# Where weight tiles wait before their conversion: other buffers, a filter load in four pieces, one write for two

## The chip, the cores and the metric

The kernel runs on one core of a Trainium2 chip. The metric is the device time of one execution in microseconds; a time given for a kernel is the median of several runs.

## What is computed

For 8 sequences of 3008 rows and 256 columns, a real Fourier transform along the rows, a product with a complex filter, the inverse transform, and then an MLP mixer over rows (token part) and columns (channel part):

```python
X = np.fft.rfft(x, axis=1)                      # x: (8, 3008, 256)
Y = X * (filt_r + 1j * filt_i)[None, :, :]      # 1505 x 256
x = np.fft.irfft(Y, n=3008, axis=1)             # float32
xt = x.transpose(0, 2, 1)
h = np.maximum(xt @ w_tok1, 0.0) @ w_tok2       # 3008 x 256, 256 x 3008
u = x + h.transpose(0, 2, 1)
out = u + np.maximum(u @ w_ch1, 0.0) @ w_ch2    # 256 x 1536, 1536 x 256
```

x and the filter are float32. The four weights are float64, and the kernel reads their bits.

## The kernel before

**The transform.** 3008 is 47 x 64, so the transform is done in two steps, each a matmul with a constant table. In `a_unit` (L283) two of 47 row groups of one batch are multiplied with the table wa, copied from PSUM by ScalarE (ACT) and written to a buffer in DRAM, z_tmp. In `b_unit` (L314), one of 32 frequencies k2 is read back (tile t2), multiplied with its table, and VectorE (DVE) makes the six operations of the complex product with the filter (L322 to L327). `bi_unit` (L330) does the first inverse step, ACT copies it to a tile t3, and t3 is written to a second buffer in DRAM, g_tmp. All of this is `dft` (L290), a generator that gives back control after each unit. The batches go in groups, `GROUPS`: batch 0 alone, then pairs.

**The mixer.** `mix` (L442) loads g_tmp as t4 tiles of four row groups, ends the inverse transform (L369) with a copy by DVE to a tile y (L372), does the token part with w1 and w2, and then twelve channel blocks for each of six row blocks (L404, L424). While a batch is mixed, the next group's `dft` runs between its steps.

**The weights.** A float64 number is made a float32 of equal value by `rounded` (L194) from its two 32-bit words: an ACT operation (L198), four DVE operations (L199, L200, L202, L204) and one sum per destination (L206). L204 is the last to read the staged words. There are 40 steps: 12 for w_tok1 (`w1_load`, two DMAs each), 16 for w_tok2 (`w2_load`), 6 for w_ch1 and 6 for w_ch2. Each is a generator in two halves: the first takes a staging tile and issues the load on POOL's queue, the second converts. `weights` (L252) runs the first halves of `AHEAD` = 5 steps, and then converts step i and issues step i + 5 in turn. A second token weight is reordered as it is written: three sums at L206, two of 23 row groups (184 columns) and one of the last row group (8 columns).

**Staging tiles** hold 128 x 512 eight-byte words, 4 KB a partition. They come from pool `t4p`, tag "t4", which has A // TC4 + 1 = 7 buffers; the mixer's t4 tiles come from the same pool and tag, six for a batch. Pools `up` (two buffers, tag "u"), `t2p` (three, "t2") and `t3p` (two, "t3") have tiles of 4 KB a partition too. A buffer is given to a new tile in the order of the program, and the instruction that writes the new tile waits until all that read or wrote the old one have ended.

**The order of the start** is written out by hand, at the end of the kernel. DVE clears the filter's tile `filt` (L475). `next(convert)` issues the loads of the first five steps, then `filt_load` (L173) issues eight DMAs on POOL's queue that gather the filter's rows: for the real and the imaginary part one of 24 partitions, two in falling order of rows (16 and 7 partitions), one for k2 = 0. Then batch 0's `dft` runs, and each of its first twelve units (the `a_unit`s) is followed by one conversion step. When it has ended, six `t4_load`s for batch 0 are issued on SP's queue, and then all conversions that are left, before the first `mix`:

```python
        for c in range(A // TC4):
            t4_load(0, c)
        for _ in convert:
            pass
```

Each engine takes its instructions in the order of the program, and so do the queues of SP, ACT and POOL.

Of the kernel before, what the change touches and what calls it, by code (L numbers as in the profile page):

```python
# [11 lines left out]
I64 = mybir.dt.int64  # L12
# [7 lines left out]
N1 = 47  # L20
N2 = 64
NF = N // 2 + 1
D = 256
P = 128
K2 = 32
A = 24
KR = 4 * A
HALF = 64
# [6 lines left out]
TC = DT // P  # L35
DC = 1536
JT = DC // P
DH = D // P
MT = 6
NG = 8  # L40
AHEAD = 5
GROUPS = ((0,), (1, 2), (3, 4), (5, 6), (7,))


# [65 lines left out]
def kernel(  # L110
# [11 lines left out]
    nc = tc.nc  # L122
# [12 lines left out]
    def pool(name, bufs, **kw):  # L135
        return ctx.enter_context(tc.tile_pool(name=name, bufs=bufs, **kw))
# [6 lines left out]
    t2p = pool("t2p", 3)  # L143
    pp = pool("pp", 2)
    t3p = pool("t3p", 2)
    t4p = pool("t4p", A // TC4 + 1)
    yp = pool("yp", 2)
    h1p = pool("h1p", 1)
    up = pool("up", 2)
# [12 lines left out]
    filt = glob.tile([P, K2, D], FP32, name="filt")  # L162
    w1 = glob.tile([P, A, DT], FP32, name="w1")
    w2 = glob.tile([P, TC, N], FP32, name="w2")
# [5 lines left out]
    def raw(src, row, ap):  # L170
        return bass.AP(tensor=src.tensor, offset=src.offset + row * D, ap=ap)

    def filt_load():  # L173
        for src, p0 in ((filt_r, 0), (filt_i, HALF)):
            nc.gpsimd.dma_start(filt[p0:p0 + A].rearrange("p a d -> p (a d)"),
                                raw(src, 0, [[64 * D, A], [1, K2 * D]]))
            lo = p0 + 32

            for j0, n in ((0, 16), (16, A - 1 - 16)):
                nc.gpsimd.dma_start(filt[lo + j0:lo + j0 + n, 1:K2, :],  # L180
                                    raw(src, 63 + 64 * j0, [[64 * D, n], [-D, K2 - 1], [1, D]]))
            nc.gpsimd.dma_start(filt[lo:lo + A, 0, :], raw(src, 32, [[64 * D, A], [1, D]]))

    def stage(n):
        return t4p.tile([P, n], I64, tag="t4", name="st")

    def rounded(st, n, parts):

        words = [st.bitcast(t).rearrange("p (n w) -> p n w", w=2)[:, 0:n] for t in (U32, FP32)]
        lo, hi, hi_f = words[0][:, :, 0], words[0][:, :, 1], words[1][:, :, 1]
        top = hp.tile([P, 512], FP32, tag="hh", name="top")[:, 0:n]
        rest = hp.tile([P, 512], FP32, tag="hh", name="rest")[:, 0:n]  # L194
        top_i, rest_i = top.bitcast(U32), rest.bitcast(U32)


        nc.scalar.activation(out=top, in_=hi_f, func=AF.Copy, scale=2.0 ** -112)  # L198
        nc.vector.tensor_scalar(out=top_i, in0=top_i, scalar1=3, scalar2=None, op0=ALU.logical_shift_left)  # L199
        nc.vector.scalar_tensor_tensor(out=top_i, in0=hi, scalar=0x80000000, in1=top_i,  # L200
                                       op0=ALU.bitwise_and, op1=ALU.bitwise_or)
        nc.vector.tensor_scalar(out=rest_i, in0=top_i, scalar1=0xFF800000, scalar2=None, op0=ALU.bitwise_and)  # L202

        nc.vector.scalar_tensor_tensor(out=rest, in0=lo, scalar=2.0 ** -52, in1=rest, op0=ALU.mult, op1=ALU.mult)  # L204
        for src, dst in parts:
            nc.vector.tensor_tensor(out=dst, in0=src(top), in1=src(rest), op=ALU.add)  # L206

    def w1_load(i):
        st = stage(512)
        rows = moe_w_tok1.rearrange("(n2 n1) t -> n2 n1 t", n1=N1)  # L210
        last = 2 * i + 2 == A
        if last:
            nc.gpsimd.memset(st.bitcast(U32)[HALF:P, 512:1024], 0)
        for h in range(2):
            n = 1 if last and h else 2
            lo = h * A + 2 * i
            nc.gpsimd.dma_start(st[h * HALF:(h + 1) * HALF, 0:n * DT].rearrange("p (a t) -> p a t", t=DT),
                                rows[:, lo:lo + n, :])
        yield
        rounded(st, 512, [(lambda v: v, w1[:, 2 * i:2 * i + 2, :].rearrange("p a t -> p (a t)"))])  # L220

    def w2_load(i):

        t, g = divmod(i, N2 // NG)
        n = NG * N1
        st = stage(512)
        nc.gpsimd.dma_start(st[:, 0:n], moe_w_tok2[ts(t, P), ts(g, n)])
        yield

        def some(lo, w):  # L230
            return lambda v: v.rearrange("p (n2 n1) -> p n1 n2", n1=N1)[:, lo:lo + w, :]

        w = A - 1
        dst = w2[:, t, 0:w * P].rearrange("p (a n2) -> p a n2", n2=P)
        rounded(st, n, [(some(h * A, w), dst[:, :, ds(h * HALF + g * NG, NG)]) for h in range(2)]
                + [(some(w, 1), w2[:, t, ds(w * P + g * NG, NG)].unsqueeze(1))])

    def wc1_load(i):
        c, q = divmod(i, DC // 512)
        st = stage(512)  # L240
        nc.gpsimd.dma_start(st, moe_w_ch1[ts(c, P), ts(q, 512)])
        yield
        rounded(st, 512, [(lambda v: v, wc1[:, c, ts(q, 512)])])

    def wc2_load(i):
        st = stage(512)
        nc.gpsimd.dma_start(st.rearrange("p (j d) -> p j d", d=D),
                            moe_w_ch2[ts(i, 2 * P), :].rearrange("(j p) d -> p j d", p=P))
        yield
        rounded(st, 512, [(lambda v: v, wc2[:, 2 * i:2 * i + 2, :].rearrange("p j d -> p (j d)"))])  # L250

    def weights():  # L252

        steps = ([w1_load(i) for i in range(A // 2)] + [w2_load(i) for i in range(TC * N2 // NG)]
                 + [wc1_load(c * (DC // 512) + q) for q in range(DC // 512) for c in range(DH)]
                 + [wc2_load(i) for i in range(JT // 2)])
        for s in steps[0:AHEAD]:
            next(s)
        yield
        for i, s in enumerate(steps):  # L260
            next(s, None)
            if i + AHEAD < len(steps):
                next(steps[i + AHEAD])
            yield


# [90 lines left out]
    t4 = {}  # L357

    def t4_load(b, c):
        t4[b, c] = t4p.tile([P, TC4, D], FP32, tag="t4", name="t4")  # L360
        nc.sync.dma_start(t4[b, c], rows_of(g_d, b)[:, ts(c, TC4), :])
# [80 lines left out]
    def mix(b, next_ready):  # L442
        h1 = token_hidden(b)
        wait = []
        uts, pos, hhs = {}, {}, {}

        def u_part(m, dh):
            if dh == 0:
                uts[m] = up.tile([P, DH, 512], FP32, tag="u", name="u")
            u_unit(b, m, h1, uts[m], dh)  # L450
            if dh == DH - 1 and b + 1 < B:
                wait.append(m)

        for dh in range(DH):
            u_part(0, dh)
        items = [(m, jt) for m in range(MT) for jt in range(JT)]
        for i in range(len(items) + 2):
            if i < len(items):
                m, jt = items[i]
                hhs[i] = hidden(uts[m], jt, width(m))  # L460
                if m + 1 < MT and jt in (5, 7):
                    u_part(m + 1, (jt - 5) // 2)
            if next_ready():
                for c in wait:
                    t4_load(b + 1, c)
                wait.clear()
            yield
            if i >= 2:
                m, jt = items[i - 2]
                down(b, m, jt, hhs.pop(i - 2), uts[m], pos.setdefault(m, []))  # L470

    with tc.manual_schedule():
        nc.sync.dma_start(wa, wa_d)
        nc.vector.memset(xlast[HALF:P, XC - 1, :], 0.0)
        nc.vector.memset(filt, 0.0)  # L475
        convert = weights()
        next(convert)
        filt_load()
        for i, _ in enumerate(dft(GROUPS[0])):
            if i == 0:  # L480
                for t, src in ((wai, wai_d), (ident, id_d)):
                    nc.scalar.dma_start(t, src)
            if i < A // 2:
                next(convert)
# [4 lines that stand above are left out]
        for bs, after in zip(GROUPS, GROUPS[1:] + ((),)):  # L489
            todo = dft(after) if after else iter(())  # L490
            done = not after
            for b in bs:
                def next_ready():
                    return b != bs[-1] or done

                for i, _ in enumerate(mix(b, next_ready)):
                    if not done and i % len(bs) == 0:
                        done = next(todo, "end") == "end"
            for _ in todo:
                raise AssertionError("the filter's steps don't fit beside the mixer's")  # L500
# [30 lines left out]
```

## Time and profile before

| | |
|---|---|
| median of 3 runs | 3232.15 us (3232.03 to 3232.48) |
| profiled execution: time | 3230.55 us |
| profiled execution: span | 3228.7 us |
| PE busy | 2941.8 us, 91% of the span |
| DVE busy | 843.9 us, 26% |
| ACT busy | 532.0 us, 16% |
| POOL busy | 134.7 us, 4% |
| mean granted TensorE clock | 0.999 |

The profile is one execution. Its span runs from the first to the last instruction, its time is the device time of the same execution, and the 1.85 us between them lie before and behind. The shares are averages over the whole span: the start, up to the first matmuls of the first `mix`, is told apart from the rest by windows of time. In rows of a timeline the first number is the start in us from the span's start, the second the duration, and the bracket at the end gives the engine's idle time before the row and what ended it. In a group of instructions the figures behind the bar are the busy time in us and the mean of one instruction in ns. An engine's name with a q (SPq, POOLq) is its queue's own work, issuing a DMA.

### The profile page before, as it was taken

The page shows a single profiled execution, that of the slowest core. Times are in us where ns is not written, and L with a number is a line of the kernel's source. Part 1 is how long each engine was busy: PE and PEld are TensorE (multiplying, and loading weights), DVE is VectorE, ACT ScalarE, POOL GpSimd, SP SyncE. Part 2 cuts the span into 40 slices and gives each one's busy share as a digit, 9 for nine tenths or more (in the row PEclk, how much of TensorE's full clock was granted, in tenths as well). Part 3 has the DMA queues.
Part 4 walks back from the last instruction along what each step waited for, and adds up shares of the span by engine and source line. Part 5 has one row for each costly group of instructions (what it writes and reads, how often), then busy time and mean ns, then how long its engine had stood idle before and what let it go on. Part 6 is the DMA issues. An engine that isn't in the chain of part 4 may idle for free.

```text
span 3228.7 us, 26261 instructions
## 1 busy us (share of the span) xinstructions
PE 2941.8 (91%) x10624; PEld 1876.0 (58%) x10624; DVE 843.9 (26%) x1442; ACT 532.0 (16%) x929; POOL 134.7 (4%) x257
## 2 busy tenths in 40 slices
PE   3610699999999999999999999999999999999999
PEld 0300466566666566666666566666666666666665
DVE  4954204751001434401001434401023330001000
ACT  1110022221121111111121111111111111111111
POOL 2000000000000000000000000000000000000000
PEclk9999999999999999999999999999999999999999
DMA  9332132330221212110221202110211101000000
GB/s 218 111 94 66 46 111 89 95 117 19 81 88 56 62 31 69 55 48 19 81 89 56 62 31 68 56 47 19 74 52 55 42 25 44 20 13 1 13 14 13
DMA packets 125096, 189.31 MB, mean 59 GB/s; under 512 B 16280, under 2 KB 84248, under 8 KB 124928
## 3 DMA queue, kind: packets, MB, share of 16 engines
q1 hardware_dynamic: 69520, 90.80, 9.4%
q0 software_dynamic: 14720, 46.35, 5.7%
q10 hardware_dynamic: 40736, 50.48, 4.7%
q8 instruction: 85, 1.39, 0.2%
q14 instruction: 35, 0.29, 0.0%
HBM read 112.59 MB, written 74.97 MB: 58 GB/s over the span
## 4 chain that ended last, share of the span: by engine, by line
PE 88%; DMA 5%; DVE 5%; issue 1%; ACT 1%; SPq 0%; POOL 0%; ACTq 0%; POOLq 0%
PE ps_po L424 31%; PE ps_pg L404 30%; PE ps_acc L378 5%; PE ps_acc L392 5%; PE ps_b L316 3%; PE ps_i L332 3%; PE ps_po L422 3%; PE ps_acc L397 3%; PE ps_a L369 3%; PE ps_a L285 2%; DMA x<-in_x_dram 2%; DMA st<-in_moe_w_ch_dram 1%; DMA st<-in_moe_w_tok_dram 1%; DVE rest L204 1%; DVE top L200 1%
## 5 line engine op out<-in xcount | busy, mean ns | idle before, releaser
L424 PE MATMUL ps_po<-wc,hh 128*128 128x256 f32 (+1 forms) x4608 | 1128.0, 381 | 0.0
L404 PE MATMUL ps_pg<-u,wc 128*128 128x512 f32 (+1 forms) x2304 | 1069.9, 587 | 0.0
L424 PEld LDWEIGHTS ps_po<-wc,hh 128*128 128x128 f32 (+1 forms) x4608 | 836.1, 188 | 311.2 <-issue 231.9
L407 ACT ACTIVATE hh<-ps_pg 128x512 f32<-128x512 f32 (+1 forms) x576 | 338.7, 588 | 1910.1 <-PE ps_pg L404 1844.0
L404 PEld LDWEIGHTS ps_pg<-u,wc 128*128 128x128 f32 x2304 | 430.5, 190 | 327.3 <-issue 296.4
L399 DVE COPY u<-ps_acc 128x512 f32<-128x512 f32 (+1 forms) x96 | 65.3, 680 | 792.3 <-PE ps_acc L397 792.3
L369 PE MATMUL ps_a<-t,wai 128*128 128x512 f32 x192 | 100.9, 607 | 182.9 <-DVE y L372 175.9
L440 POOL DMA_DIRECT2D out_dram<-o x192 | 100.1, 528 | 2781.1 <-ACT o L436 2730.8
L322 DVE TENSOR_TENSOR p<-ps_b,filt 64x512 f32<-64x512 f32 (+1 forms) x144 | 85.5, 594 | 437.2 <-PE ps_b L316 436.7
L392 PE MATMUL ps_acc<-w,h 128*128 128x512 f32 (+1 forms) x384 | 178.7, 588 | 11.8 <-DVE u L399 6.3
L436 DVE COPY o<-ps_po 128x512 f32<-128x512 f32 x40 | 27.6, 691 | 613.1 <-PE ps_po L424 613.0
L378 PE MATMUL ps_acc<-y,w 128*128 128x256 f32 x768 | 181.7, 381 | 0.0
L378 PEld LDWEIGHTS ps_acc<-y,w 128*128 128x128 f32 x768 | 147.1, 192 | 58.3 <-issue 42.7
L332 PE MATMUL ps_i<-p,wi 128*96 128x512 f32 (+1 forms) x320 | 153.7, 565 | 24.3 <-DVE p L327 14.5
L369 PEld LDWEIGHTS ps_a<-t,wai 128*128 128x128 f32 x192 | 36.3, 193 | 195.6 <-DVE y L372 183.3
L316 PE MATMUL ps_b<-t,wb 96*128 96x512 f32 (+1 forms) x288 | 134.9, 551 | 9.3 <-DMA t<-z_tmp 9.3
L422 PEld LDWEIGHTS ps_po<-ident,u 128*128 128x128 f32 (+1 forms) x768 | 114.3, 189 | 30.5 <-issue 23.1
L392 PEld LDWEIGHTS ps_acc<-w,h 128*128 128x128 f32 x384 | 71.6, 190 | 99.0 <-issue 80.6
L397 PEld LDWEIGHTS ps_acc<-wai,t 128*128 128x128 f32 x768 | 100.8, 192 | 44.2 <-issue 44.2
L422 PE MATMUL ps_po<-ident,u 128*128 128x128 f32 (+1 forms) x768 | 117.0, 275 | 0.0
L336 ACT COPY t<-ps_i 96x512 f32<-96x512 f32 (+1 forms) x160 | 79.4, 496 | 218.5 <-PE ps_i L332 216.2
L332 PEld LDWEIGHTS ps_i<-p,wi 128*96 128x96 f32 x320 | 54.1, 181 | 98.6 <-issue 93.4
(53 smaller groups left out, 1151.2 us busy)
## 6 DMA issues: line engine op xcount, KB each, us to landing
z_tmp<-t ACTq DMA_DIRECT2D x96, 256.0 KB, 2.5
t<-z_tmp SPq DMA_DIRECT2D x128, 192.0 KB, 3.4
g_tmp<-t ACTq DMA_DIRECT2D x128, 192.0 KB, 3.2
t<-g_tmp SPq DMA_DIRECT2D x48, 512.0 KB, 5.1
out_dram<-o POOLq DMA_DIRECT2D x184, 128.0 KB, 2.5
x<-in_x_dram SPq DMA_DIRECT2D x176, 128.0 KB, 3.3
wb<-wb_t SPq DMA_DIRECT2D x80, 96.0 KB, 2.0
wi<-wi_t SPq DMA_DIRECT2D x80, 96.0 KB, 2.0
```

The source lines that it names most:

```text
L316: nc.tensor.matmul(ps, wbs[k // WC][:, k % WC, :], t2s[k // KC][:, k % KC], start=True, stop=True)
L322: nc.vector.tensor_tensor(out=p1[re], in0=ps[re], in1=fr, op=ALU.mult)
L332: nc.tensor.matmul(ps[0:KR], wis[k // WC][:, k % WC, :], prods.pop(k), start=True, stop=True)
L369: nc.tensor.matmul(ps, wai, t4[b, c * XC // TC4][:, ds(c * XC % TC4, XC), :].rearrange("p a d -> p (a d)"), start=True, stop=True)
L378: nc.tensor.matmul(acc[:, t, :], w1[:, a, ts(t, P)], y[:, r, :], start=(a == 0 and t == 0), stop=(a == A - 1 and t == TC - 1))
L392: nc.tensor.matmul(ps[:, 0:w], h1[:, t, ts(dh, P)], w2[:, t, ds(m * 512, w)], start=(t == 0), stop=False)
L397: nc.tensor.matmul(ps[:, ds(q * P, n)], t4[b, c][:, r, ts(dh, P)], wai[:, 0:n], start=False, stop=(q == 3))
L404: nc.tensor.matmul(ps[:, 0:w], wc1[:, c, ts(jt, P)], ut[:, c, 0:w], start=(c == 0), stop=(c == DH - 1))
L407: nc.scalar.activation(out=hh[:, 0:w], in_=ps[:, 0:w], func=AF.Relu)
L422: nc.tensor.matmul(ps[:, ts(dh, P)], ut[:, dh, ds(q * P, n)], ident, start=(q % 2 == 0 and dh == 0), stop=False)
L424: nc.tensor.matmul(ps, hh[:, ds(q * P, n)], wc2[:, jt, :], start=False, stop=(end and q in (1, 2)))
L440: nc.gpsimd.dma_start(rows[:, lo:lo + n, :], o[h * HALF:(h + 1) * HALF, 0:n, :])
```

## The change

Four edits, all in the start of the kernel.

- `stage` takes its tiles from a list: the 12 first token weights from "t4" as before, then two from "u", then 26 from "t2" and "t3" by turns.
- `AHEAD` is 6 instead of 5, and `weights` is split: beside the first twelve conversions only steps up to 13 are issued (the first two second token weights); four more are issued after batch 0's spectral part and its t4 loads, and from there on step i + 6 is issued behind the conversion of step i.
- `filt_load` takes a range of k2 and is called four times by `weights`, for 8 values of k2 each, behind the conversions 0, 2, 4 and 6: eight DMAs for the first piece, six for each other.
- `w2_load` writes both runs of 23 row groups by one operation with a longer access pattern; the one for the last row group stays.

```diff
-AHEAD = 5
+AHEAD = 6
...
-    def filt_load():
+    def filt_load(k0, nk):
         for src, p0 in ((filt_r, 0), (filt_i, HALF)):
-            nc.gpsimd.dma_start(filt[p0:p0 + A].rearrange("p a d -> p (a d)"),
-                                raw(src, 0, [[64 * D, A], [1, K2 * D]]))
+            nc.gpsimd.dma_start(filt[p0:p0 + A, k0:k0 + nk, :], raw(src, k0, [[64 * D, A], [D, nk], [1, D]]))
             lo = p0 + 32
+            if k0 == 0:
+                nc.gpsimd.dma_start(filt[lo:lo + A, 0, :], raw(src, 32, [[64 * D, A], [1, D]]))
+            k = max(k0, 1)
 
             for j0, n in ((0, 16), (16, A - 1 - 16)):
-                nc.gpsimd.dma_start(filt[lo + j0:lo + j0 + n, 1:K2, :],
-                                    raw(src, 63 + 64 * j0, [[64 * D, n], [-D, K2 - 1], [1, D]]))
-            nc.gpsimd.dma_start(filt[lo:lo + A, 0, :], raw(src, 32, [[64 * D, A], [1, D]]))
+                nc.gpsimd.dma_start(filt[lo + j0:lo + j0 + n, k:k0 + nk, :],
+                                    raw(src, 64 * (j0 + 1) - k, [[64 * D, n], [-D, k0 + nk - k], [1, D]]))
+
+    stages = ([(t4p, "t4")] * (A // 2) + [(up, "u")] * 2
+              + [((t2p, "t2"), (t3p, "t3"))[i % 2] for i in range(TC * N2 // NG + JT - 2)])
 
     def stage(n):
-        return t4p.tile([P, n], I64, tag="t4", name="st")
+        where, tag = stages.pop(0)
+        return where.tile([P, n], I64, tag=tag, name="st")
...
         w = A - 1
-        dst = w2[:, t, 0:w * P].rearrange("p (a n2) -> p a n2", n2=P)
-        rounded(st, n, [(some(h * A, w), dst[:, :, ds(h * HALF + g * NG, NG)]) for h in range(2)]
-                + [(some(w, 1), w2[:, t, ds(w * P + g * NG, NG)].unsqueeze(1))])
+        dst = w2[:, t, 0:w * P].rearrange("p (a h n2) -> p h a n2", h=2, n2=HALF)
+
+        def both(v):
+            return bass.AP(tensor=v.tensor, offset=v.offset, ap=[v.ap[0], [A, 2], [1, w], [N1, NG]])
+
+        rounded(st, n, [(both, dst[:, :, :, ds(g * NG, NG)]), (some(w, 1), w2[:, t, ds(w * P + g * NG, NG)].unsqueeze(1))])
...
+        n1 = A // 2
         for s in steps[0:AHEAD]:
             next(s)
         yield
-        for i, s in enumerate(steps):
+        for i, s in enumerate(steps[0:n1]):
             next(s, None)
-            if i + AHEAD < len(steps):
+            if i + AHEAD < n1 + 2:
                 next(steps[i + AHEAD])
+            if i % 2 == 0 and i < 8:
+                filt_load(4 * i, 8)
+            yield
+        for s in steps[n1 + 2:n1 + AHEAD]:
+            next(s)
+        for i, s in enumerate(steps[n1:]):
+            next(s, None)
+            if n1 + i + AHEAD < len(steps):
+                next(steps[n1 + i + AHEAD])
             yield
...
         convert = weights()
         next(convert)
-        filt_load()
```

## The prediction

> **What bounds the kernel now.** I read the page's busy slices first, then busy time by 40 us windows, then the stretch where TensorE does nothing.
>
> ```profile
> span 3228.7 us, 26261 instructions
> PE   3610699999999999999999999999999999999999
> 0.00:40.00 40.00, 10.22 (x10) 2.50 (x10) 15.85 (x17) 5.94 (x9) 11.61 (x25) 1.00 1.00 181
> 40.00:80.00 40.00, 14.07 (x14) 3.58 (x14) 22.77 (x41) 9.69 (x16) 9.60 (x18) 1.00 0.98 252
> 80.00:120.00 40.00, 25.80 (x52) 14.00 (x52) 35.50 (x83) 4.41 (x12) 0.00 (x0) 1.00 0.37 113
> 240.00:280.00 40.00, 0.00 (x0) 0.00 (x0) 16.76 (x38) 2.93 (x5) 3.20 (x6) 1.00 0.23 66
> 360.00:400.00 40.00, 38.53 (x142) 25.34 (x141) 7.60 (x11) 3.29 (x6) 0.00 (x0) 1.00 0.06 19
> ```
>
> The windows give, behind the stretch, the busy time of PE, PEld, DVE, ACT and POOL with their instructions, the granted clock, the busy share of the DMA engines and GB/s. From about 350 us on TensorE is full and stays so; the change touches nothing there. Ahead of it lie three stages with three limits: to about 82 us the DMA engines are full (share 1.00 and 0.98), to about 172 us DVE is (35.5 of 40 us, the filter's products), and from there to 352 us nothing is: DVE 16.8 of 40, DMA 0.23, TensorE nothing. The timeline of DVE gives the edges, and the chain of waits shows what the third stage is made of.
>
> ```profile
> 85.91 0.42 DVE L322 TENSOR_TENSOR p<-ps_b,filt 64x256 f32<-64x256 f32 x1 [2.40 <-PE ps_b L316]
> ...
> 171.20 0.42 DVE L327 TENSOR_TENSOR p<-p,p 64x256 f32<-64x256 f32 x1
> 174.32 0.36 DVE L199 TENSOR_SCALAR top<-top 128x376 uint32<-128x376 uint32 x1 [2.70 <-ACT top L198]
> ...
> 176.27 0.92 DVE L206 TENSOR_TENSOR w<-top,rest 128x184 f32<-128x184 f32 x3
> 177.12 0.35 DVE L199 TENSOR_SCALAR top<-top 128x376 uint32<-128x376 uint32 x1
> ...
> 351.70 0.68 DVE L372 COPY y<-ps_a 128x512 f32<-128x512 f32 x1
> ```
>
> ```profile
> 195.40 0.56 DVE rest L204
> 195.99 0.51 issue
> 196.50 3.32 DMA st<-in_moe_w_tok_dram
> 199.90 0.55 ACT top L198
> ...
> 201.87 0.56 DVE rest L204
> ...
> 342.68 0.70 DVE rest L204
> ...
> 343.92 4.02 DMA st<-in_moe_w_ch_dram
> 348.02 0.67 ACT top L198
> ...
> 350.36 0.70 DVE rest L204
> ```
>
> One weight tile follows the other: DVE's last read of the staged tile (L204), half a microsecond, the next tile's load, ACT's and DVE's conversion, the next last read. A turn is 201.87 - 195.40 = 6.5 us for a second token weight and 350.36 - 342.68 = 7.7 us for a channel weight. The reason is in the code: a staged tile and the mixer's t4 tiles share seven buffers, six are given to batch 0's t4 loads before the remaining conversions, and one is left to rotate. POOL's timeline agrees: its first load of this stage waited 110 us and was released by a conversion's L204.
>
> ```profile
> 187.93 0.54 POOL L227 DMA_DIRECT2D st<-in_moe_w_tok_dram  x1 [109.98 <-DVE rest L204]
> ```
>
> **Term 1, the staging.** The stage converts 16 second token weights and 12 channel weights from 174.32 to 351.70, that is 177.4 us. After the change the tiles lie in two u buffers, three t2 and two t3 buffers, whose owners are idle between batch 0's spectral part and the mixer's first batch. Two tiles wait in u before the stage begins. The third and the fifth need t2 buffers whose last reader is TensorE, ahead of the last products at 171 us; the fourth and sixth need t3 buffers, free when their writes to DRAM have landed, a few us after those products, and they are due only three and five steps, 8 and 13 us, into the stage. From then on tile n needs the buffer of tile n-6 (t2) or n-4 (t3). The tighter one decides: from the last read of n-4 to the first DVE operation of n there are four pitches less the 1.9 us from the start of a conversion to the end of its L204 (174.32 to 176.27, where L206 begins), so 4 x 2.7 - 1.9 = 8.9 us. A load needs, by the turn above, from L204's end at 195.96 to ACT's end at 200.45, 4.5 us (5.3 for a channel weight, 343.38 to 348.69). That leaves 3.6 us or more: DVE no longer waits, and the stage lasts as long as DVE's work. If the cover went, by a landing of more than 4.0 + 3.6 = 7.6 us, each four steps would pay the excess.
>
> What a step costs DVE without waiting: 177.12 - 174.32 = 2.80 us for a second token weight. For a tile of 512 columns the first weights, which run the same five operations, show it back to back:
>
> ```profile
> 67.83 0.42 DVE L199 TENSOR_SCALAR top<-top 128x512 uint32<-128x512 uint32 x1
> 68.17 0.54 POOL L227 DMA_DIRECT2D st<-in_moe_w_tok_dram  x1 [1.03 <-DVE w L206]
> 70.81 0.42 DVE L199 TENSOR_SCALAR top<-top 128x512 uint32<-128x512 uint32 x1
> ```
>
> 2.98 us. ACT's part (0.55, 0.67) runs a step ahead on its own engine.
>
> **Term 2, one write for two.** Two operations of 184 columns become one of 368; the one of 8 stays.
>
> ```profile
> L206 DVE TENSOR_TENSOR w<-top,rest 128x184 f32<-128x184 f32 x32 | 13.5, 465 | 0.5
> L206 DVE TENSOR_TENSOR wc<-top,rest 128x512 f32<-128x512 f32 x12 | 8.3, 691 | 0.4
> L206 DVE TENSOR_TENSOR w<-top,rest 128x8 f32<-128x8 f32 x16 | 2.7, 166 | 0.0
> ```
>
> From 8 to 184 columns the strided operation grows by 299 ns, 1.70 ns a column; by that the merged one is 166 + 360 x 1.70 = 778 ns instead of 2 x 465 = 930, but neighbours overlap (465 + 465 + 166 = 1.10 us of work took 0.92, so 0.09 at each of two seams) and one seam goes, which leaves 0.06 us. By the contiguous row (691 ns for 512 columns, 1.04 ns a column) it would be 541 ns and the saving 0.3 us. The trace has no operation with so long an access pattern; I let a penalty take it to -0.1. I take 0.06, because the strided row is the same access: 2.74 us a step. Sixteen steps: 1 us, bounds -1.6 and 5.
>
> The stage is then 16 x 2.74 + 12 x 2.98 = 79.6 us instead of 177.4: 97.8 us less. At its end the same first y copy follows. Batch 0's t4 loads no longer compete for buffers; the spectral part keeps DVE's 85.7 us (85.91 to 171.62).
>
> **Term 3, the first stage.** The load of the filter becomes 26 DMAs instead of 8 and moves behind the loads of first weights, on POOL's queue; three of five second token weights leave the stage.
>
> ```profile
> DMA packets 7797, 18.19 MB, mean 214 GB/s; under 512 B 1455, under 2 KB 2523, under 8 KB 7747
> st<-in_moe_w_tok_dram POOLq DMA_DIRECT2D x23, 256.0 KB, 11.6
> st<-in_moe_w_tok_dram POOLq DMA_DIRECT2D x5, 376.0 KB, 7.5
> filt<-in_filt_i_dram POOLq DMA_DIRECT2D x1, 217.0 KB, 37.1
> ...
> 1.28 4.28 POOL L217 DMA_DIRECT2D st<-in_moe_w_tok_dram  x8 [0.82 <-POOLq L515]
> 6.02 0.52 POOL L217 DMA_DIRECT2D st<-in_moe_w_tok_dram  x1 [0.46 <-DMA st<-in_moe_w_tok_dram]
> ...
> 20.31 0.53 POOL L182 DMA_DIRECT2D filt<-in_filt_i_dram  x1 [1.94 <-DMA st<-in_moe_w_tok_dram]
> ...
> 55.31 1.02 POOL L217 DMA_DIRECT2D st<-in_moe_w_tok_dram  x2 [2.33 <-DMA filt<-in_filt_i_dram]
> ```
>
> The first four rows are of the DMA view from 0 to 85 us (count, KB each, us to landing), the others POOL's timeline. With the engines full, bytes set the stage: 3 x 376 KB = 1.16 MB less, at the stage's mean of 214 GB/s 5.4 us, at the 252 of its second half 4.6. I take 5. The filter's bytes are the same; what pieces do to their rate this trace does not show, so I bound it. Better: between 20 and 50 us, where the filter passes, six windows of 5 us move 104, 122, 135, 211, 150 and 155 GB/s, and 253 before them.
>
> ```profile
> 15.00:20.00 5.00, 1.50 (x2) 0.00 (x0) 1.90 (x4) 0.00 (x0) 1.91 (x3) 1.00 1.19 253
> 20.00:25.00 5.00, 0.00 (x0) 0.00 (x0) 0.00 (x0) 0.00 (x0) 0.53 (x1) 1.00 0.99 104
> ...
> 45.00:50.00 5.00, 2.05 (x2) 0.50 (x2) 0.00 (x0) 0.00 (x0) 0.51 (x1) 1.00 0.90 155
> ```
>
> At 253 the same 4.4 MB would take 17 us instead of 30, so 13 us more gain. Worse: POOL has at most eight loads in flight (eight leave at once, the ninth waits for a landing). Before, 24 + 8 + 5 = 37 loads pass, after 24 + 26 + 2 = 52; if a landing stays at 11.6 us whatever the size, 15 x 11.6 / 8 = 22 us are added. I stay with bytes, as the share of the DMA engines is full throughout, and count the extra issues (0.5 us each of POOL, which idles) at nothing. The pieces are due at the spectral part's units 0, 8, 16 and 24, spaced 8 x 2.7 us, and none is near its time.
>
> The Trainium skill, DMA: Bandwidth & Descriptors, "Anatomy of one DMA", puts a fixed cost of about 2 us on each DMA and so speaks against pieces: 18 more would be 36 us one behind another, or 4.5 us with eight in flight; by the latter the sum below would come to 99 instead of 103. The trace shows the eight in flight, so the former can't be the case.
>
> **The sum.** 98 + 5 = 103 us. The profiled execution took 3230.55 us (span 3228.7), 1.6 below the median of 3232.15; it gives 3127.5, and as a median of runs 3129.
>
> **The rivals.** (a) The pieces mix better with x and first weights: 13 us more, 3116. For it: engines full at half the rate. Against: the same few partitions are written. Chance 0.13. (b) The eight in flight bind: 22 us on top, no 5 saved: 3156 at the end, 3129 to 3156 on the way. For it: POOL waits for landings in the whole stage. Against: less in flight lands sooner. Chance 0.13. (c) POOL's loads cannot be prepared while DVE works without pause: the six staged tiles are used up, DVE waits 4.5 us, and so on; 22 further tiles in groups of six are 3.7 waits, 17 us: 3146. Against it: the POOL row at 68.17 stands inside a dense DVE step, takes 0.54 like the one at 187.93 beside an idle DVE, and the step keeps its 2.98. Chance 0.05. The Trainium skill, SBUF — State Buffer, "SBUF: two separate sides", states such a lock between VectorE and GpSimd's descriptors; by that row the trace doesn't show it here. (d) Slower: each filter piece stands in POOL's queue ahead of a first weight that ACT must convert before it copies the next x unit. If a piece landed as late as the whole does (37.1 us), four would take 148 us where the filter now takes 35 (20.31 to 55.31): 113 lost, 98 won, 3247. It decides from (98 + 35) / 4 = 33 us a piece. For it: 37.1 us for 217 KB is queue, not bytes. Against: that queue was the filter itself. Chance 0.02. (e) The change doesn't do what it says: the t2 or t3 buffers come free too late or are rotated one at a time, and the third stage keeps its turns: 3227 to 3232. The code gives five buffers by turns; chance 0.02.
>
> **How the numbers follow.** The likeliest case has the rest, 0.65: 3129, by itself 3122 to 3136. The range 3115 to 3144 takes in (a) and the near half of (b), and leaves out the far half, most of (c), (d) and (e): under 2 in 10. About 0.2% is what a measurement of this kernel can tell from no change, 6.5 us. Faster beyond it: all but (d) and (e), 0.96; same 0.02, slower 0.02.
>
> **What would show it.** DVE without gaps from the end of the spectral part (about 169 us) to the first y copy near 249, steps of about 2.7 and 2.98 us; POOL's loads there issued in bunches and not each released by the L204 just before; one L206 of 368 columns near 0.78 us; the first L322 near 81 us instead of 85.91; from the first y copy on the same 2877 us to the end. Wrong would be: gaps of DVE released by loads of st in that stage (c, e), or a first L322 at 90 us or later (b, d) or at 72 or earlier (a).

## The result, and the profile after

The changed kernel takes 3117.07 us (median of 4 runs, 3114.72 to 3118.63) against 3232.32 of the kernel before (4 runs): ratio 0.9642, 95% interval 0.9626 to 0.9659. Forecast were 3129 and a range of 3115 to 3144. The gain is 115 us where 103 were expected; the sign, the main term and its size held, the third term was three times as large.

The profiled execution took 3114.72 us, its span is 3112.9. The windows of the start answer to those of before (busy time of PE, PEld, DVE, ACT and POOL, granted clock, DMA share, GB/s):

```profile
0.00:40.00 40.00, 17.82 (x18) 4.30 (x18) 25.24 (x34) 9.57 (x15) 19.18 (x38) 0.98 0.98 255
40.00:80.00 40.00, 14.19 (x22) 5.88 (x22) 27.14 (x54) 7.29 (x13) 11.00 (x19) 0.50 0.77 203
80.00:120.00 40.00, 29.87 (x60) 16.01 (x60) 37.73 (x90) 5.51 (x15) 0.00 (x0) 0.50 0.35 105
160.00:200.00 40.00, 2.07 (x2) 0.50 (x2) 38.04 (x88) 8.24 (x15) 7.00 (x14) 0.50 0.71 239
200.00:240.00 40.00, 1.63 (x2) 0.84 (x3) 36.57 (x66) 7.36 (x11) 5.96 (x9) 0.50 0.35 123
240.00:280.00 40.00, 38.53 (x145) 27.15 (x144) 8.98 (x13) 0.60 (x1) 0.00 (x0) 0.96 0.00 0
```

The third stage has a limit now: DVE is busy 38.0 and 36.6 of 40 us where it was 16.8. And the first stage moves 255 GB/s in its first 40 us where it moved 181, at the same full share of the DMA engines. DVE's timeline gives the edges (L340, L345, L204, L211 and L390 are L322, L327, L199, L206 and L372 of before):

```profile
69.25 0.42 DVE L340 TENSOR_TENSOR p<-ps_b,filt 64x256 f32<-64x256 f32 x1 [6.49 <-PE ps_b L334]
...
154.62 0.42 DVE L345 TENSOR_TENSOR p<-p,p 64x256 f32<-64x256 f32 x1
157.74 0.36 DVE L204 TENSOR_SCALAR top<-top 128x376 uint32<-128x376 uint32 x1 [2.70 <-ACT top L203]
...
159.69 0.86 DVE L211 TENSOR_TENSOR w<-top,rest 128x368 f32<-128x368 f32 x2
160.47 0.38 DVE L204 TENSOR_SCALAR top<-top 128x376 uint32<-128x376 uint32 x1
...
237.63 0.68 DVE L390 COPY y<-ps_a 128x512 f32<-128x512 f32 x1
```

Between the two profiles the span is 115.8 us shorter (3228.7 to 3112.9), and it parts so: the first filter product 16.7 us earlier (85.91 to 69.25); from there to the first conversion no change (88.41 and 88.49 us); the conversions 97.5 us shorter (177.38 to 79.89); from the first y copy to the end 1.7 us shorter (2877.0 to 2875.3). POOL's timeline of the third stage shows the loads in pairs, each pair released by one L209 (L204 of before), some 5.5 us apart, which is two conversions:

```profile
168.43 1.06 POOL L232 DMA_DIRECT2D st<-in_moe_w_tok_dram  x2 [7.73 <-DVE rest L209]
173.94 1.06 POOL L232 DMA_DIRECT2D st<-in_moe_w_tok_dram  x2 [4.45 <-DVE rest L209]
179.47 1.06 POOL L232 DMA_DIRECT2D st<-in_moe_w_tok_dram  x2 [4.46 <-DVE rest L209]
```

Why the pieces of the filter were worth 12 us more than forecast was the open question. One theory was bytes (three weight tiles fewer), the rivals were the form of the transfers, their size and their place.

### The profile page after: what moved, and what is told of

The parts are those of the page before. It is cut to its first block, busy times and chain, and to the rows that moved or that the text cites. A ratio compares the mean times of both kernels' runs of the same rounds, so it can differ in the third digit from the quotient of the medians.

```text
span 3112.9 us, 26266 instructions
## 1 busy us (share of the span) xinstructions
PE 2941.5 (94%) x10624; PEld 1876.1 (60%) x10624; DVE 841.6 (27%) x1426; ACT 532.3 (17%) x929; POOL 145.3 (5%) x275
## 2 busy tenths in 40 slices
DMA packets 125576, 189.31 MB, mean 61 GB/s; under 512 B 16616, under 2 KB 84584, under 8 KB 125264
## 4 chain that ended last, share of the span: by engine, by line
PE 92%; DVE 5%; DMA 2%; issue 1%; ACT 0%; POOL 0%; POOLq 0%; ACTq 0%; SPq 0%; DVEq 0%
PE ps_po L442 33%; PE ps_pg L422 32%; PE ps_acc L396 5%; PE ps_acc L410 5%; PE ps_b L334 3%; PE ps_i L350 3%; PE ps_po L440 3%; PE ps_acc L415 3%; PE ps_a L387 3%; PE ps_a L303 2%; DMA st<-in_moe_w_tok_dram 1%; DMA z_tmp<-t 1%; DVE rest L209 1%; DVE top L205 1%; DVE p L343 0%
## 5 line engine op out<-in xcount | busy, mean ns | idle before, releaser
L458 POOL DMA_DIRECT2D out_dram<-o x192 | 100.1, 528 | 2782.8 <-ACT o L454 2771.0
L340 DVE TENSOR_TENSOR p<-ps_b,filt 64x512 f32<-64x512 f32 (+1 forms) x144 | 85.5, 594 | 441.3 <-PE ps_b L334 440.8
L387 PE MATMUL ps_a<-t,wai 128*128 128x512 f32 x192 | 100.9, 607 | 85.4 <-DVE y L390 78.6
L415 PEld LDWEIGHTS ps_acc<-wai,t 128*128 128x128 f32 x768 | 100.8, 192 | 44.2 <-issue 44.2
L390 DVE COPY y<-ps_a 128x512 f32<-128x512 f32 x96 | 66.3, 691 | 164.5 <-PE ps_a L387 163.8
```

The lines of the kernel that those rows point to most:

```text
L340: nc.vector.tensor_tensor(out=p1[re], in0=ps[re], in1=fr, op=ALU.mult)
L387: nc.tensor.matmul(ps, wai, t4[b, c * XC // TC4][:, ds(c * XC % TC4, XC), :].rearrange("p a d -> p (a d)"), start=True, stop=True)
L415: nc.tensor.matmul(ps[:, ds(q * P, n)], t4[b, c][:, r, ts(dh, P)], wai[:, 0:n], start=False, stop=(q == 3))
L458: nc.gpsimd.dma_start(rows[:, lo:lo + n, :], o[h * HALF:(h + 1) * HALF, 0:n, :])
```

## The experiments

Where a run has several times, its difference is to the kernel before on the same chip. The first filter product of one profile is a figure with a spread: four profiles of kernels whose first stage is the same (the changed one, the one with three sums, the one with two buffers, the one with the mixer beside) have it at 69.2, 70.7, 72.8 and 73.3 us, and four that load the filter whole, told below, at 82.0 to 85.0. Differences of less than 4 us in it say nothing by themselves.

**Whole filter, old place.** The staging is new, the load of the filter old.

```diff
-            if i % 2 == 0 and i < 8:
-                filt_load(4 * i, 8)
...
         next(convert)
+        filt_load()
```

> The changed kernel, but the filter is loaded whole by its old eight DMAs, ahead of the first weights' conversions as before. In question is why the first filter product (L322 before, L340 after) came 16.7 us earlier (85.91 to 69.2 us) where 5 were forecast. Bytes alone (three second token weights fewer in this stage): it stays near 69 us, total near 3117. The filter's form or place: near 81 us (85.9 less the 5 of the bytes), total near 3129. Either way the conversions behind the spectral part stay at 80 us without gaps.

3128.50 us (4 runs), before 3229.86: ratio 0.9688, 0.9674 to 0.9703. First product at 83.5 us, conversions 79.9 us. The new staging (with the merged write) gives 101 us without the pieces. The first product comes 2.4 us earlier than before; that is less than the spread, so it doesn't size the bytes of three weight tiles, but it is far from 16.7. Form or place of the load makes the rest.

**All pieces, old place.**

```diff
         next(convert)
+        for k0 in range(0, K2, 8):
+            filt_load(k0, 8)
```

> The changed kernel, but all four filter pieces (26 DMAs) are issued at the old place, ahead of all conversions. If the form of the pieces (shorter runs, no 32 KB packets in the way of the x units) made the gain: first product near 69 to 72 us, total near 3117 to 3120. If their place between the first weights did: near 81 us, total near 3129. If the number of DMAs in flight binds, later than that, near 90.

3121.44 us (4 runs), ratio 0.9667, 0.9652 to 0.9681; first product at 75.6 us. So 26 DMAs instead of 8 at the same place win 8 us in the profile and 7 in time (3128.50 to 3121.44, on the same chip). The place between the first weights' conversions wins 2 to 6 more by the profiles, which the spread leaves open; the run with three sums, which has the pieces there, is 4.7 us faster on the same chip, but it was timed once.

**Only the filter.** The kernel before with the pieces between the conversions.

```diff
                 next(steps[i + AHEAD])
+            if i % 2 == 0 and i < 8:
+                filt_load(4 * i, 8)
             yield
...
-        filt_load()
```

> The kernel before with the filter in four pieces between the conversions and nothing else: old staging, AHEAD 5, three sums. If the filter's form or place makes the other 12 us: first product near 74 us, total near 3220. If the gain comes from fewer bytes: near 86, total near 3232. The third stage keeps its turns of 6.5 and 7.7 us.

3217.62 us (5 runs), ratio 0.9961, 0.9947 to 0.9975: 12.2 us less, by itself. First product at 77.6 us, 8.3 earlier than before; the rest of the profile's gain of 11.7 us is not in the first stage: the conversions take 175.15 us instead of 177.38, for which no run shows a reason, and the time behind the first y copy is 1.3 us shorter, which is taken up below. With the 101.4 of the staging the two parts sum to 113.6 of the whole change's 115.3.

The windows from 10 to 60 us show what the pieces do. First the kernel before, then the one with the whole filter at its old place, with all pieces there, and the changed one:

```profile
10.00:60.00 50.00, 15.01 (x15) 4.00 (x16) 15.68 (x28) 7.57 (x13) 10.48 (x19) 1.00 1.02 190
```

```profile
10.00:60.00 50.00, 15.68 (x16) 4.01 (x16) 17.49 (x30) 7.25 (x13) 9.56 (x17) 1.00 1.03 188
```

```profile
10.00:60.00 50.00, 18.45 (x18) 4.51 (x18) 20.27 (x35) 9.86 (x17) 21.96 (x40) 1.00 1.03 236
```

```profile
10.00:60.00 50.00, 21.91 (x22) 5.30 (x22) 32.53 (x56) 14.24 (x24) 23.97 (x42) 0.79 1.03 274
```

The share of the DMA engines is 1.02 or 1.03 in all four, what they move goes from 188 to 274 GB/s. A full share is time in which packets are under way, not a rate.

**Three sums.**

```diff
-        rounded(st, n, [(both, dst[:, :, :, ds(g * NG, NG)]), (some(w, 1), w2[:, t, ds(w * P + g * NG, NG)].unsqueeze(1))])
+        rounded(st, n, [(some(h * A, w), dst[:, :, ds(h * HALF + g * NG, NG)]) for h in range(2)]
+                + [(some(w, 1), w2[:, t, ds(w * P + g * NG, NG)].unsqueeze(1))])
```

> The changed kernel with the second token weights written by three sums as before. Step of a second token weight 2.79 us instead of 2.76; the first y copy 0.5 to 1 us later from the start of the conversions. By the contiguous row it would be 0.3 us a step, 5 us.

The conversions take 80.4 us (159.25 to 239.66) instead of 79.9: the merged operation is worth 0.5 us. In the changed kernel's groups it costs 785 ns against two of 184 columns at 465:

```profile
L211 DVE TENSOR_TENSOR w<-top,rest 128x368 f32<-128x368 f32 x16 | 12.6, 785 | 0.6
...
L211 DVE TENSOR_TENSOR w<-top,rest 128x8 f32<-128x8 f32 x16 | 2.7, 170 | 0.0
```

The longer pattern costs as much a column as the shorter one, 1.70 ns, so only one start of an operation is saved.

**Whole filter in rows of 1 KB.**

```diff
         next(convert)
+        filt_load(0, K2)
```

> As the run with the filter whole and ahead of the conversions (first product at 83.5 us), but its two DMAs of 24 partitions are written as rows of 1 KB instead of runs of 32 KB; eight DMAs, same bytes, same place. If the 32 KB runs stand in the way of the other transfers, the first product comes near 75.6 us as with the pieces at that place. If the number of pieces makes those 8 us, it stays near 83.

First product at 82.0 us, 3129.45 us (one run). The rows are only in the way the code writes the load: over the whole execution this kernel and the one with the whole filter at its old place move the same 125096 packets, 124928 of them under 8 KB. The long runs are still there, so this run does not test them and is one more measure of the whole load. The run with the pieces in another order, below, does: it moves the packets of the pieces (125576, 125264 under 8 KB) and is as slow.

**Whole filter behind the first conversion.**

```diff
-            if i % 2 == 0 and i < 8:
-                filt_load(4 * i, 8)
+            if i == 0:
+                filt_load()
```

> The changed kernel with the filter loaded whole by its old eight DMAs, but behind the first conversion, where the first piece was. If the place alone makes 6 us (75.6 to 69.2 between pieces first and pieces between): first product near 77 us. If the place helps only because pieces alternate with first weights: near 83 us.

First product at 82.8 us, 3129.05 us (one run). The place by itself is worth nothing that the spread lets one see; if it helps, it is only where pieces alternate with first weights.

**The same pieces in another order.** What is left is that pieces are smaller, or that small DMAs of different partitions follow one another. This run keeps size, number and place and changes the order alone:

```diff
+            for k0 in range(0, K2, 8):
+                nc.gpsimd.dma_start(filt[p0:p0 + A, k0:k0 + 8, :], raw(src, k0, [[64 * D, A], [D, 8], [1, D]]))
...
+            for j0, n in ((0, 16), (16, A - 1 - 16)):
+                for k0 in range(0, K2, 8):
+                    k = max(k0, 1)
+                    nc.gpsimd.dma_start(filt[lo + j0:lo + j0 + n, k:k0 + 8, :],
```

> The same 26 filter DMAs at the same place as in the run with all pieces first (first product at 75.6 us), but in another order: all that write the same partitions stand together (24 partitions of the real part four times, then its 16, its 7, then the imaginary part), as the whole filter's eight DMAs do. If what counts is that the DMAs in flight at one time write different partitions: first product near 82 us, total near 3128. If smaller DMAs by themselves make the gain: near 75.6 us, total near 3121.

3130.96 us (4 runs; before 3231.80; ratio 0.9688, 0.9672 to 0.9704), first product at 84.6 us. In the order of this run the 26 DMAs are as slow as the eight; in the other they win 8 to 9 us. By time the two orders won 108.4 and 100.8 us on their own chips, 7.6 apart; the ends of the two intervals overlap, so it is the trace that decides. The window from 10 to 60 us has the rate of the whole filter, not that of the pieces:

```profile
10.00:60.00 50.00, 16.37 (x16) 4.02 (x16) 17.48 (x30) 7.67 (x13) 17.15 (x32) 1.00 1.02 194
```

The first product does not wait for the filter itself here: DVE converts without a gap up to it. What comes late are the first weights queued behind the filter. POOL issues the first of them at these times, with all pieces first and then in this run:

```profile
45.35 0.56 POOL L222 DMA_DIRECT2D st<-in_moe_w_tok_dram  x1 [0.20 <-issue]
```

```profile
54.72 0.58 POOL L222 DMA_DIRECT2D st<-in_moe_w_tok_dram  x1 [0.39 <-DMA filt<-in_filt_i_dram]
```

The rows of the DMA view for the 24 partitions (count, KB each, us to landing), in the same order:

```profile
filt<-in_filt_r_dram POOLq DMA_DIRECT2D x4, 192.0 KB, 9.5
filt<-in_filt_i_dram POOLq DMA_DIRECT2D x4, 192.0 KB, 9.7
```

```profile
filt<-in_filt_r_dram POOLq DMA_DIRECT2D x4, 192.0 KB, 14.4
filt<-in_filt_i_dram POOLq DMA_DIRECT2D x4, 192.0 KB, 13.1
```

The pieces of 16 partitions rise likewise (9.8 and 9.6 us to 13.8 and 15.3), those of 7 don't (8.9 and 9.0, 8.4 and 9.1). So the order of the queue decides: neighbours of the same kind hold each other up where mixed ones don't. What makes them the same kind stays open. The order of this run puts pieces of the same partitions together, which read neighbouring rows in DRAM, and it also sends the 13 loads of the real part ahead of the 13 of the imaginary part, which go to the other half of the partitions and which the fast order mixes. No run parts these three.

**Without the filter.** The filter's load is left out.

```diff
-            if i % 2 == 0 and i < 8:
-                filt_load(4 * i, 8)
```

> The changed kernel without the load of the filter: it stays cleared, so the product is zero; everything else runs. It shows what the filter's 3 MB cost in the first stage. At the 255 GB/s that the stage moves with pieces, 3.0 MB are 12 us: first product near 58 to 60 us. If the stage isn't bound by bytes: near 70.

The filter's tile stays cleared, so the output isn't the product that was asked for. First product at 54.9 us, 3107.11 us (one run). The filter's 3 MB cost 14 to 18 us as the change loads them, more than the 12 expected, and 29 us (83.5 - 54.9) whole. The time shows less of it, because 10.9 us pass from the end of the last output DMA's issue to the end of the span, 3.6 in the changed kernel; no view shows why.

**Five steps ahead.**

```diff
-AHEAD = 6
+AHEAD = 5
```

> The changed kernel with five steps ahead instead of six, everything else kept. First product 69 to 73 us if the depth in the first stage costs nothing, near 76 if the first weights' loads were the late ones. The conversions behind the spectral part still take 80 us, since the tighter rule there is the four steps of the t3 buffers.

First product at 74.6 us, conversions 79.9 us, 3118.94 us (one run). The third stage doesn't need the sixth step; whether the first gains by it can't be told from one profile that lies 1.2 us outside the spread.

**Two buffers.** This tests the rule by which the prediction said that the loads are hidden.

```diff
-              + [((t2p, "t2"), (t3p, "t3"))[i % 2] for i in range(TC * N2 // NG + JT - 2)])
+              + [(t3p, "t3")] * (TC * N2 // NG + JT - 2))
```

> The changed kernel with all tiles behind the two in u staged in the two t3 buffers. By the rule of the prediction tile n waits for the last read of n-2: two steps take 1.95 + 4.5 = 6.45 us instead of 5.5 for a second token weight and 2.4 + 5.3 = 7.7 instead of 5.96 for a channel weight, so 14 x 0.47 + 12 x 0.87 = 17 us more between the first conversion and the first y copy, 97 us instead of 80. If the number of buffers isn't what counts: 80. If one tile follows the other as in the kernel before: 170.

100.1 us from the first conversion (161.31) to the first y copy (261.43), 3138.05 us (one run); 97 was forecast by the rule. The 3 us over are about what one load cost that took 7.7 us to land while SP's queue issued batch 0's six t4 loads and six x loads (162.6 to 171.9 us). The chain of waits has the loads back, that one first:

```profile
169.24 7.73 DMA st<-in_moe_w_tok_dram
...
196.34 3.49 DMA st<-in_moe_w_tok_dram
...
200.07 3.34 DMA st<-in_moe_w_tok_dram
```

**The mixer beside the conversions.** With DVE as the limit of the third stage, TensorE's next work can be put under it: batch 0's inverse transform and token part need w1 alone.

```diff
+            next(beside, None)
+            next(beside, None)
...
-        h1 = token_hidden(b)
+        h1 = token_hidden(b, convert if b == 0 else iter(()))
+        if b == 0:
+            for _ in convert:
+                pass
```

> The changed kernel, but batch 0's inverse transform and token part, which needs only w1, runs between the conversions of the second token and channel weights: each of its 13 steps is followed by two conversions. If DVE's own work bounds this stage: 80 us of conversions and 12 y copies of 0.7, 88 us up to h1 instead of 80 + 34, so some 22 to 25 us less, near 3093 us. If TensorE's clock or the copies' waits take it back: near 3117.

3096.96 us (4 runs, 3096.69 to 3097.72; before 3230.51): ratio 0.9587, 0.9571 to 0.9603, the fastest of the study. It wins 133.6 us on its chip's kernel before where the changed kernel won 115.3 on its own: 18 us more. The y copies on DVE now stand between the conversions, two conversions to a copy, and the first u copy follows the last conversion:

```profile
169.10 0.69 DVE L390 COPY y<-ps_a 128x512 f32<-128x512 f32 x1 [9.93 <-PE ps_a L387]
...
175.28 0.68 DVE L390 COPY y<-ps_a 128x512 f32<-128x512 f32 x1
181.34 0.69 DVE L390 COPY y<-ps_a 128x512 f32<-128x512 f32 x1
...
255.38 0.69 DVE L211 TENSOR_TENSOR wc<-top,rest 128x512 f32<-128x512 f32 x1
255.99 0.68 DVE L419 COPY u<-ps_acc 128x512 f32<-128x512 f32 x1
```

6.06 us a pair is two conversions of 2.7 and a copy of 0.7: from the first y copy to the first u copy (86.9 us, 88 expected) DVE has no gap, so its own work bounds the stage. Ahead of it DVE waits 9.9 us, until batch 0's t4 loads and the first inverse matmul have ended; the changed kernel fills that time with conversions after a wait of 2.7. From the last filter product to the first u copy it is 97.2 us here (158.75 to 255.99) and 120.3 in the changed kernel (154.62 to 274.91), so the stage itself gains 23 us, as expected. The whole gain is 4 us under the least expected, because in this profile the first product comes at 73.3 us, 4 us later than in the changed kernel's, within the spread of that stage, and the time behind the first u copy is 2 us longer.

**The end of POOL's queue.** The profile after is 1.7 us shorter behind the first y copy, where nothing was changed. The last output DMAs, before and after:

```profile
3220.90 0.53 POOL L440 DMA_DIRECT2D out_dram<-o  x1 [39.21 <-ACT o L436]
3224.27 1.56 POOL L440 DMA_DIRECT2D out_dram<-o  x3 [2.85 <-issue]
```

```profile
2877.45 0.53 POOL L458 DMA_DIRECT2D out_dram<-o  x1 [2.78 <-issue]
...
3106.85 1.04 POOL L458 DMA_DIRECT2D out_dram<-o  x2 [39.21 <-ACT o L454]
3108.22 1.04 POOL L458 DMA_DIRECT2D out_dram<-o  x2 [0.33 <-DVE o L452]
```

POOL stands 2.8 us near the end. Before, it falls into the last four DMAs and so into the time; after, it falls 21 DMAs ahead of the end, where POOL idles anyway. The profiles agree: behind the first y copy the five with 252 DMAs on POOL's queue (the filter whole, the next run among them) take 2876.1 to 2877.4 us, the seven with 270 that keep the mixer's order 2874.4 to 2875.7. A run took the kernel with the whole filter at its old place and put 18 small clears ahead, to move POOL's instructions and no DMA:

```diff
         nc.vector.memset(filt, 0.0)
+        for _ in range(18):
+            nc.gpsimd.memset(pad, 0.0)
```

> As the run with the filter whole and ahead of the conversions, with 18 small clears on POOL put in at the start, so that POOL has as many instructions as with the pieces. In the kernels with eight filter DMAs POOL's last three output DMAs stand 2.85 us idle for no reason that the profile shows, in those with 26 they don't. If it is the place of these instructions in POOL's stream, the gap is gone here and the time from the first y copy to the end is 2 us shorter (2875 instead of 2877 us); if it belongs to the filter's load, it stays.

The gap stayed, with three DMAs behind it:

```profile
3125.72 1.57 POOL L455 DMA_DIRECT2D out_dram<-o  x3 [2.85 <-issue]
```

So the number of POOL's instructions doesn't place it, and it isn't the old filter load either, since the changed kernel has it too, only earlier. Counted in DMAs it fits: POOL issues 252 before and 270 after, and 252 - 3 = 270 - 21 = 249. In the run without the filter, with 244 DMAs, the last groups have no such gap. The changed kernel shows the same gap once more, behind POOL's 128th DMA, far from the end:

```profile
1111.77 1.04 POOL L458 DMA_DIRECT2D out_dram<-o  x2 [2.86 <-issue]
```

What happens behind the 128th and the 249th DMA no view shows; it was not tested further.

## Why the prediction was right, and where not

**Term 1, the staging (97.8 us): right.** Measured 97.5. From its first conversion on DVE converts without a gap, at the durations that the prediction took from back-to-back rows of the profile before (2.76 and 2.98 us a step where 2.74 and 2.98 were expected), and the rule for the cover holds in the run with two buffers, where it makes the loads late by about what it says. No wait took the place of the one removed: what bounds the stage next is DVE's own work, and the run with the mixer beside shows that TensorE has room under it.

**Term 2, the merged write (1 us): right in kind.** 785 ns for 778; 0.5 us in all. The strided row, not the contiguous one, was the one to go by.

**Term 3, the first stage (5 us): mis-sized.** Measured 16.7 us in the profile, 12.6 to 16.7 over the four profiles of this stage. The step that failed is "With the engines full, bytes set the stage", and "I stay with bytes, as the share of the DMA engines is full throughout". The share was full before and after, and the rate was not: 190 and 274 GB/s. Rival (a) had this result (13 us more, 3116) with a chance of 0.13, and its sign, a first product at 72 us or earlier, came in two of the four profiles. The likeliest case by itself, 3122 to 3136, missed the time by 5 us; that the time lies in the range is owed to (a), which the range took in. The argument against (a), that the same few partitions are written, holds only for a queue in which like loads follow one another: with the pieces mixed, the same partitions are written and the first product comes 12.6 to 16.7 us earlier. The evidence lay in the profile before, in the windows of 104 GB/s at a share of 0.99; it should have been read as transfers that hold each other up, and not as a stage with a fixed rate.

The Trainium skill, SBUF — State Buffer, "Door 1: The DMA port swizzle", states that a DMA's rate depends on how many of 16 SBUF ports its partitions reach; by its formula the filter's 24, 16 and 7 partitions reach 6, 4 and 2. The slow windows fit that, though no run here shows a port, and the pieces of 7 partitions, the fewest, landed no later in the slow order. The same page's answer to "Can I just issue two DMAs to hit both halves?" is no, with 6% for two at once. No run here is that case, two loads alone; with eight in flight the two orders of the same 26 DMAs (75.6 and 84.6 us) differ by 9 us.

**The rivals.** (b) and (d) needed landings that don't shrink with the piece; the filter's DMAs took 18.9 to 37.1 us to land whole and 6.8 to 11.4 in pieces. (c) would have shown gaps of DVE in the third stage: there are none while POOL issues in pairs. (e) is excluded by the 79.9 us.

**The end** was forecast at 2877 us and measured 2875.3: the gap behind POOL's 249th DMA left the path. The prediction took the end for fixed; the 2.85 us with no releaser in the profile before were a part of it that 18 more DMAs could move.

## What to carry to other kernels

A stage in which no engine is full and the chain repeats load, convert, load was short of buffers here: look for tiles that are idle at that time, and count from which earlier tile's last read each load must wait. A full DMA share says that packets are under way, not how fast; where GB/s falls at a full share, look at what neighbouring transfers in the queue have in common, and try mixing them. When one limit goes, put the next engine's ready work under the new one.

## What the hardware showed that was not expected

The granted TensorE clock is 0.50 in the profile of the changed kernel from about 39 to 243 us and 1.00 in that of the kernel before, and the matmuls of the spectral part, which have gaps between them, take the same time. It is not the change that lowers the clock: the mean over a whole execution is about 0.967 in three runs of the changed kernel and 1.000 in one, and about 0.955 or 0.999 in runs of the kernel before. The group and the window from 90 to 150 us, before and then after:

```profile
L332 PE MATMUL ps_i<-p,wi 128*96 128x256 f32 x44 | 25.1, 673 | 15.1 <-DVE p L327 8.1 <-issue 7.1
...
90.00:150.00 60.00, 44.46 (x90) 23.51 (x88) 56.63 (x135) 8.27 (x23) 0.00 (x0) 1.00 0.37 109
```

```profile
L350 PE MATMUL ps_i<-p,wi 128*96 128x256 f32 x45 | 25.8, 674 | 15.9 <-DVE p L345 8.8 <-issue 7.1
...
90.00:150.00 60.00, 44.09 (x90) 23.70 (x90) 56.56 (x135) 8.09 (x22) 0.55 (x1) 0.50 0.36 107
```

673 ns at the full granted clock and 674 at half (by ends that the profile models), and the same 88.4 and 88.5 us for the stage: here the granted clock has no bearing on the time. By 244 us, with TensorE full, it is back at 1.00. The recorded durations don't tell what the clock does to a matmul: in the run with the mixer beside, two of L387 took 2.08 us at 0.50 (at 200.35 us) and 1.12 us at 1.00 (at 206.45 us), but 2.07 us at 1.00 too (at 166.99 us).
